# Side sums taken by turns on VectorE, a narrower last convolution block on TensorE, and other rounds with bank halves

## The chip, the cores and the metric

The kernel runs on one core of a Trainium2 chip. The metric is the time of one execution on the device in microseconds (us), lower is better. Three runs of the kernel before were timed; their median is 510.24 us.

## What is computed

A causal convolution along the sequence, with softmaxed taps of 7 per head (8 heads of 24 columns, D = 192), feeds a multiplicative feed-forward network:

```python
w = softmax(weight)                                   # H=8 heads, K=7 taps
out = np.einsum('hk,bskhg->bshg', w, x_unf)           # x_unf[t, k] = x[t - 6 + k], zeros ahead of a batch
a = out @ w1                                          # 192 -> 1024
b = out @ w2
return ((a * b) @ w3) @ w_out                         # 1024 -> 1024 -> 192
```

There are 8 batches of 3904 tokens, 31232 rows in all. The kernel multiplies `w3 @ w_out` once, so a row needs two products to 1024 columns, an elementwise product, and one product back to 192.

## The kernel before, in words

**Streams, rounds, stages.** The rows are cut into two streams of 15616, which share the 128 partitions (64 columns of D each). A round R is 512 tokens of both streams; there are 31. Three rounds make a stage (`phases`): first the *first products* of its three rounds, then their *second products*, two a round (one for each stream), six in all. Stage 0 holds rounds 0 to 2, stage 9 the first products of 27 to 29 and the second ones of 27, a last stage the rest.

- A first product (`first_product`) has eight steps. In each, TensorE makes `pa` and `pb` (six matmul pairs of 64 rows each, line 633), ScalarE copies `pa` to `asb` (line 640), and VectorE multiplies `asb` with `pb` to `abT` (line 643).
- A second product (`second_product`) is 32 matmuls of 128 rows (line 685) into one pair of banks, `ops`; ScalarE copies it to `osb` (line 690) and SyncE's queue sends it out.
- All PSUM tiles are pairs of banks from one ring of four, so the third `pb` of a stage waits until VectorE has read the first.

**Halves.** In stages 3, 6, 7 and 8 (`halves`) the two second products of a round are made by `half_rows` in matmuls of 64 rows, two at a time (line 664): the first half of both products, then the second half of both, with the banks changed over. Between the halves a no-operation on VectorE (`passed`, line 674) waits for the first half's last matmul, and the second half waits for it. So both products of a round are done late in it: the first after three quarters.

**Where the convolution is done.** D is three column groups k of 64. The tokens of rounds 2q+1 and 2q+2 form pair q. For q in `SIDE` (4, 5, 8, 9, 12, 13, 14) all three groups are convolved aside: VectorE, and for some halves GpSimd, multiplies and adds seven shifted copies, group by group. In `PART` (10 and 11) group 0 alone is made aside. All else TensorE convolves with banded matrices (`conv`, line 345), ScalarE copies the result out (line 355), it is stored to DRAM and read back transposed. Blocks 4, 5 and 6 are convolved between the second products, in units of up to two heads (`units`, `places`): four units in stage 0, four in stage 2, three (heads 2 to 7 of block 6) in stage 5. A unit of two heads is 32 matmuls.

**A side task** is (q, k, tokens). Its rows are cast to bf16 by GpSimd's DMA queue (`side_cast`), read back transposed on SyncE's queue (`side_transpose`, five buffers in turn), scaled by the tap of shift 1 on ScalarE (`side_first`, line 520; the *first scaling*), and then VectorE adds the six other shifts (`side_sums`, line 538; the *sums*), each 1024 elements wide, or 768 for q = 14. There are two accumulators: task i takes `acc_of[i % 2]`, so its first scaling waits for the last sum of task i - 2. Sums all add to the task's own accumulator. If a batch starts within the task, the sums are split there.

**GpSimd's half tasks** (`POOL_AT`) work alike on 512 tokens; where a stage has two of them, ScalarE does their first scalings (`pool_first`, line 571) in the stage before, around its fifth second product.

**The order.** VectorE, ScalarE and the queues take their instructions in program order. A planner spreads the sums over the stages: `rooms` says how many a stage takes, `steps` is the list of all sums, task by task, and `chain[p]` becomes stage p's list, with each first scaling put at a number n. `side_steps(p, n, ...)`, called after each second product, issues what is due. So VectorE's queue holds in a stage 24 products of line 643, then the stage's sums, then the next stage's products. ScalarE's holds 24 copies of line 640, then evictions of line 690, evictions of the convolution, first scalings and GpSimd's first scalings in program order, then the next stage's copies. In halves, the sums are also portioned out around VectorE's no-operations (`limit`).

Of the kernel before, what the change touches and what calls it, by code (L numbers as in the profile page):

```python
# [16 lines left out]
def kernel(  # L17
# [32 lines left out]
    PART = {10: (0,), 11: (0,)}  # L50
# [418 lines left out]
    def half_of(q, h):  # L469
# [4 lines left out]
               5: ((8, 2, 1), (11, 0, 0)), 6: ((12, 2, 0), (11, 0, 1)), 7: ((12, 2, 1),),  # L474
# [11 lines left out]
    def side_tiles():  # L486
# [8 lines left out]
        for i, q in enumerate(SIDE):  # L495
            side_of[q] = (a if i % 2 == 0 else b)[:, 0:NP * 2 * CH].rearrange(
                "p (k t) -> p k t", k=NP)
# [26 lines left out]
    def side_sums(i):  # L524
# [4 lines left out]
        def job(d, last):  # L529
            def run():  # L530
# [4 lines left out]
                for lo, hi in [(t0, t1)] if last else \  # L535
# [3 lines left out]
                        out=side_of[p][:, k, o:o + t1 - t0] if last else a,  # L539
# [3 lines left out]
        size = (t1 - t0) / (2 * CH)  # L543
# [10 lines left out]
    def part_tile():  # L554
        t = work.tile([128, XN], BF16, tag="xb", bufs=5, name="side")
        o = 0
        for q, ks in PART.items():
            n = len(ks) * 2 * CH
            side_of[q] = t[:, o:o + n].rearrange("p (k t) -> p k t", k=len(ks))
            o += n  # L560
# [14 lines left out]
    def pool_sums(lane, own, p, k, half):  # L575
        _, _, t0, starts = pool_half(p, k, half)

        def job(d):
            def run():
# [9 lines left out]
                if d == 0:  # L589
                    o = half * CH  # L590
                    nc.gpsimd.tensor_tensor(out=side_of[p][:, k, o:o + CH], in0=acc, in1=tmp,
# [9 lines left out]
    def operand(R, k, rs):  # L601
        if beside(phase_of(R), k):
            t0 = R * CH - side_span(phase_of(R))[0]
            return side_of[phase_of(R)][rs, k, t0:t0 + width(R)]
# [68 lines left out]
    def passed(mm):  # L673
        relay = nc.vector.nop()
# [125 lines left out]
    starts, chain, begun, room, p = {}, {}, set(), 0, -1  # L800
    for i, cost, f in steps:
        while room < cost:
# [4 lines left out]
        if i not in begun:  # L807
            begun.add(i)
            starts[p].append(i)
            n = max(p == 0, int(at) // 2 - 1, -(-ends.get(i - 2, 0) // 2))  # L810
# [4 lines left out]
        ends[i] = at  # L815
    for p in starts:
        for i in starts[p]:
            assert i < 5 or p < 2 or max(v for v in chain if chain[v][0][0] <= i - 5) <= p - 1

    def side_steps(p, n, state, limit=100):  # L820
        items = chain.get(p, [])
        done = sum(items[v][3] for v in state)
        for v, (i, at, f, cost) in enumerate(items):
            if at is not None and at <= n and v not in state:
# [221 lines left out]
```

## Time and profile before

| | |
|---|---|
| median of 3 runs | 510.24 us (509.89 the lowest) |
| the profiled execution | 510.52 us, of which its span is 508.8 |
| granted TensorE clock | 0.999 |

The rows of the page and of the chain of waits that matter are shown in the prediction. In the page's first part each engine has its busy time, its share of the span and its number of instructions; the chain shows what ended last, followed back. In a timeline each row is a start, a length, the engine, the line, what is written and read, and a count where like instructions follow each other; a bracket gives the idle time before, and who ended it. All times are in us from the start of the span.

### The profile page before, as it was taken

The page shows a single profiled execution, that of the slowest core. Times are in us where ns is not written, and L with a number is a line of the kernel's source. Part 1 is how long each engine was busy: PE and PEld are TensorE (multiplying, and loading weights), DVE is VectorE, ACT ScalarE, POOL GpSimd, SP SyncE. Part 2 cuts the span into 40 slices and gives each one's busy share as a digit, 9 for nine tenths or more (in the row PEclk, how much of TensorE's full clock was granted, in tenths as well). Part 3 has the DMA queues.
Part 4 walks back from the last instruction along what each step waited for, and adds up shares of the span by engine and source line. Part 5 has one row for each costly group of instructions (what it writes and reads, how often), then busy time and mean ns, then how long its engine had stood idle before and what let it go on. Part 6 is the DMA issues. An engine that isn't in the chain of part 4 may idle for free.

```text
span 508.8 us, 15240 instructions
## 1 busy us (share of the span) xinstructions
PE 503.7 (99%) x6500; PEld 336.5 (66%) x6500; DVE 446.3 (88%) x402; ACT 349.1 (69%) x390; POOL 255.7 (50%) x340
## 2 busy tenths in 40 slices
PE   8999999999999999999999999999999999999997
PEld 4546865595569557845874596569457855975697
DVE  7898769999999799999999998999999999999930
ACT  6786667746779776577567778763776477457752
POOL 8875201332890799499879944992371056000000
PEclk9999999999999999999999999999999999999999
DMA  9999979999969858970997097619402500240025
GB/s 136 152 173 157 176 151 180 151 164 173 175 41 165 150 144 112 227 120 13 92 234 109 4 166 142 130 23 182 111 1 72 162 1 1 65 125 1 1 66 156
DMA packets 161121, 58.57 MB, mean 115 GB/s; under 512 B 116896, under 2 KB 161052, under 8 KB 161052
## 3 DMA queue, kind: packets, MB, share of 16 engines
q0 software_dynamic: 74784, 17.37, 37.9%
q1 hardware_dynamic: 86107, 40.12, 37.2%
q8 instruction: 51, 0.84, 0.6%
q14 instruction: 19, 0.15, 0.1%
q10 hardware_dynamic: 160, 0.10, 0.1%
HBM read 35.02 MB, written 34.85 MB: 137 GB/s over the span
## 4 chain that ended last, share of the span: by engine, by line
PE 98%; ACT 0%; DVE 0%; issue 0%
PE pa L633 31%; PE pb L633 31%; PE ops L685 19%; PE ops L664 12%; PE cps L345 1%; PE wps L757 1%; PE warm L246 1%; PE tps L420 0%; PE ops L710 0%; DVE abT L643 0%; PE tps L435 0%; PE cps L375 0%; ACT asb L640 0%; ACT convo L355 0%; PE bps L305 0%
## 5 line engine op out<-in xcount | busy, mean ns | idle before, releaser
L643 DVE TENSOR_TENSOR abT<-asb,pb 128x1024 bf16<-128x1024 bf16 x240 | 292.6, 1220 | 28.9 <-ACT asb L640 12.8
L640 ACT CAST asb<-pa 128x1024 bf16<-128x1024 f32 x244 | 247.0, 1012 | 64.0 <-PE pa L633 63.8
L633 PEld LDWEIGHTS <-wn 64*128 64x128 bf16 x1488 | 138.8, 94 | 81.3 <-issue 0.9
L633 PEld LDWEIGHTS <-ws 64*128 64x128 bf16 x1488 | 130.4, 94 | 70.7 <-issue 0.9
L633 PE MATMUL pb<-xT,wn 64*128 64x512 bf16 x376 | 103.7, 376 | 0.0
L633 PE MATMUL pa<-xT,ws 64*128 64x512 bf16 x376 | 103.5, 376 | 0.0
L690 ACT COPY osb<-ops 128x768 f32<-128x768 f32 (+1 forms) x61 | 48.4, 795 | 80.0 <-PE ops L685 42.9
L633 PE MATMUL pa<-xT,wn 64*128 64x512 bf16 x376 | 102.9, 376 | 0.1
L633 PE MATMUL pb<-xT,ws 64*128 64x512 bf16 x376 | 102.2, 376 | 0.0
L633 PE MATMUL pb<-side,wn 64*128 64x512 bf16 (+1 forms) x368 | 100.5, 369 | 0.0
L685 PE MATMUL ops<-W_sb,abT 128*128 128x192 bf16 x1168 | 99.5, 246 | 0.0
L633 PE MATMUL pa<-side,wn 64*128 64x512 bf16 (+1 forms) x368 | 99.3, 369 | 0.0
L633 PE MATMUL pa<-side,ws 64*128 64x512 bf16 (+1 forms) x368 | 99.3, 369 | 0.0
L685 PEld LDWEIGHTS <-abT 128*128 128x128 bf16 x1168 | 95.4, 98 | 4.6 <-issue 4.6
L633 PE MATMUL pb<-side,ws 64*128 64x512 bf16 (+1 forms) x368 | 98.2, 369 | 0.0
L538 DVE SCALAR_TENSOR_TENSOR acc<-raw,wC,acc 128x1024 f32<-128x1024 bf16 (+2 forms) x70 | 84.5, 1208 | 2.3 <-PE ops L664 0.2
L596 POOL TENSOR_TENSOR acc<-acc,tmp 128x512 f32<-128x512 f32 (+6 forms) x60 | 70.3, 1176 | 4.3
L584 POOL TENSOR_TENSOR tmp<-acc,wC 128x512 f32<-128x512 bf16 x66 | 68.5, 1038 | 3.5
L664 PE MATMUL ops<-W_sb,abT 64*128 64x192 bf16 x1536 | 64.2, 243 | 0.4 <-issue 0.4
L664 PEld LDWEIGHTS <-abT 64*128 64x128 bf16 x1536 | 63.5, 94 | 1.5 <-issue 0.6
L951 POOL COPY pace<-abT 1x2 bf16<-1x2 bf16 x28 | 4.9, 174 | 109.4 <-DVE abT L643 109.3
L506 POOL DMA_DIRECT2D rows_c<-in_x_dram x58 | 40.7, 710 | 6.3 <-issue 5.5
(85 smaller groups left out, 247.0 us busy)
## 6 DMA issues: line engine op xcount, KB each, us to landing
out_dram<-osb SPq DMA_DIRECT2D x54, 384.0 KB
xb<-in_x_dram POOLq DMA_DIRECT2D x16, 240.0 KB, 7.3
out_dram<-osb SPq DMA_DIRECT2D x12, 192.0 KB
rows_c<-in_x_dram POOLq DMA_DIRECT2D x14, 130.0 KB, 6.7
rows_c<-in_x_dram POOLq DMA_DIRECT2D x14, 128.0 KB, 5.9
xb<-in_x_dram POOLq DMA_DIRECT2D x6, 228.0 KB, 8.8
w3b<-in_moe_w_dram POOLq DMA_DIRECT2D x4, 256.0 KB, 5.6
w3b<-in_moe_w_dram POOLq DMA_DIRECT2D x8, 128.0 KB, 4.9
```

Source lines behind the costliest of these rows:

```text
L246: nc.tensor.matmul(t[:, j % 2, 0:wd].rearrange("p (a c) -> p a c", c=128), zeros, zeros.unsqueeze(1).to_broadcast([128, wd // 128, 128]), ...
L345: nc.tensor.matmul(o.rearrange("p (w g) -> p w g", g=wd)[:, :, c - c0:c1 - c0], Aband[group(r, e), h, :], xb[group(r, e), s:s + m, c:c1], ...
L506: nc.gpsimd.dma_start(out=rows_c[lo:t1, k, r * Q:r * Q + Q], in_=x_rows[r * TS + lo:r * TS + t1, k * Q:k * Q + Q])
L538: nc.vector.scalar_tensor_tensor(out=side_of[p][:, k, o:o + t1 - t0] if last else a, in0=raw[:, HALO + lo - t0 - d:HALO + hi - t0 - d], sc ...
L584: nc.gpsimd.tensor_tensor(out=acc if d == 1 else tmp, in0=pool_raw[lane][:, HALO - d:HALO - d + CH], in1=wC[:, k, K - 1 - d:K - d].to_broa ...
L596: nc.gpsimd.tensor_tensor(out=a, in0=a, in1=tmp[:, lo - t0:hi - t0], op=ALU.add)
L633: nc.tensor.matmul(p[:, r, f * N:f * N + N], w_of(i, k, r)[rs, ft * 128:(ft + 1) * 128], operand(R, k, rs), start=(k == 0), stop=(k == NP ...
L640: nc.scalar.copy(out=asb[:, :, 0:per * N], in_=pa[:, :, 0:per * N])
L643: nc.vector.tensor_tensor(out=ab[:, f0, :, 0:N], in0=asb[:, :, 0:N], in1=pb[:, :, 0:N], op=ALU.mult)
L664: mm = nc.tensor.matmul(ops[:, a, g * D:g * D + D], ab[rs, jt, r, q * 128:(q + 1) * 128], W_sb[rs, jt, :], start=(turn == 0 and g == 0 and ...
L685: nc.tensor.matmul(ops[:, g // 2, (g % 2) * D:(g % 2) * D + D], ab[:, jt, r, g * 128:(g + 1) * 128], W_sb[:, jt, :], start=(jt == 0), stop ...
L690: nc.scalar.copy(out=osb.rearrange("p (a g) d -> p a (g d)", g=2), in_=ops[:, 0:ng // 2, 0:2 * D])
```

## The change

- `PART` holds groups 0 and 1 of pairs 10 and 11: tasks (10, 1) and (11, 1) go to VectorE, twelve sums more. Block 6 is then convolved by TensorE for heads 5 to 7 alone, in units of two heads and one, in places 1 and 3 of stage 5.
- The second half of (13, 2) goes from VectorE to GpSimd, in stage 7, which then has two half tasks.
- The sums are no longer listed task by task: the even and the odd tasks make two lists, which are taken by turns, by what each has spent. `rooms` is new (15 in stage 2, 14 in stage 5, else about 13), and a first scaling's number n comes from 1.2 us a sum and 2.66 a second product.
- The bank turn's no-operation (`passed`) moves from VectorE to ScalarE; `side_steps` loses its `limit`.
- Halves are used in stages 6 to 9 and in the last round of stages 2 and 5; not in stage 3.
- In halves, GpSimd's first scalings are issued after the eviction of the fifth second product, no longer ahead of it.
- The side results of pairs 10 and 11 take two tiles (`part_tile(3)` in stages 3 and 6).

```diff
-    PART = {10: (0,), 11: (0,)}
+    PART = {10: (0, 1), 11: (0, 1)}
...
-               5: ((8, 2, 1), (11, 0, 0)), 6: ((12, 2, 0), (11, 0, 1)), 7: ((12, 2, 1),),
+               5: ((8, 2, 1), (11, 0, 0)), 6: ((12, 2, 0), (11, 0, 1)), 7: ((12, 2, 1), (13, 2, 1)),
...
-    for q in SIDE:
-        for k in range(NP):
+    for q in sorted(SIDE + tuple(PART)):
+        for k in PART.get(q, range(NP)):
...
-        size = (t1 - t0) / (2 * CH)
+        size = (t1 - t0 + 130) / (2 * CH + 130)
...
     def passed(mm):
-        relay = nc.vector.nop()
+        relay = nc.scalar.nop()
...
-    places = {0: (1, 2, 3, 4), 2: (0, 1, 2, 3), 5: (0, 1, 3)}
-    rooms = (6, 12, 12, 12, 12, 12, 12, 11.25, 12)
-    steps = [(i, cost, f) for i in range(len(tasks)) for cost, f in side_sums(i)]
-    late_sum = max(v for v, (i, _, _) in enumerate(steps) if tasks[i][:2] == (12, 0))
+    places = {0: (1, 2, 3, 4), 2: (0, 1, 2, 3), 5: (1, 3)}
+    rooms = (6, 12, 15, 13, 13, 14, 13, 12.7, 13)
+    lines = [[(i, cost, f) for i in range(c, len(tasks), 2) for cost, f in side_sums(i)]
+             for c in range(2)]
+    spent, steps = [0, rooms[0]], []
+    while any(lines):
+        c = min((c for c in range(2) if lines[c]), key=lambda c: (round(spent[c], 2), c))
+        steps.append(lines[c].pop(0))
+        spent[c] += steps[-1][1]
+    late_sum = max(v for v, (i, _, _) in enumerate(steps) if tasks[i][:2] == (14, 0))
...
-            n = max(p == 0, int(at) // 2 - 1, -(-ends.get(i - 2, 0) // 2))
+            n = max(p == 0, int((1.2 * ends.get(i - 2, -1) + 1.2) / 2.66))
...
+    units = [(b, h, min(n, H - h)) for b, h, n in units]
...
-        if p == 3:
-            part_tile()
+        if p in (3, 6):
+            part_tile(3)
...
-        halves = p in (3, 6, 7, 8)
-        side_steps(p, 0, state, 0 if halves else 100)
+        side_steps(p, 0, state)
         for n, (R, r) in enumerate((R, r) for R in ends for r in range(NS)):
+            halves = p in (6, 7, 8, 9) or p in (2, 5) and R == ends[-1]
             if halves and r == 0:
                 opss = [banks("ops") for _ in range(NS)]
                 mms = [half_rows(R, i, opss[i], 0) for i in range(NS)]
-                relays = []
-                for i in range(NS):
-                    side_steps(p, n, state, 2 * n + i)
-                    relays.append(passed(mms[i]))
+                relays = [passed(mm) for mm in mms]
                 for i in range(NS):
                     half_rows(R, i, opss[i], 1, relays[i])
-                side_steps(p, n, state, 2 * n + 2)
-                side_steps(p, n + 1, state, 2 * n + 4)
-            own_first = n == 4 and len(pool_from.get(p, ())) > 1
-            if own_first and halves:
-                for lane, t in enumerate(pool_from[p]):
-                    pool_first(lane, *t)
...
-                second_product(R, r, results if p == 0 else None, opss[r])
-            if own_first and not halves:
+                second_product(R, r, results if p == 0 else None, opss[r] if halves else None)
+            if n == 4 and len(pool_from.get(p, ())) > 1:
                 for lane, t in enumerate(pool_from[p]):
                     pool_first(lane, *t)
             if n in places.get(p, ()):
                 convolve(p)
-            side_steps(p, n + 1, state, 2 * n + 2 if halves and n < 5 else 100)
+            side_steps(p, n + 1, state)
```

With these lists the stages hold (task.shift; F is a first scaling, with its n): stage 2: F4, F3 at 0, tasks 4 and 3 by turns (12 sums), F6 at 5, 6.2, F5 at 5, 5.2, 6.3. Stage 3: nine sums of 5 and 6, F8 at 4, 8.2, F7 at 4, 7.2, 8.3, 7.3. Stage 4: eight of 8 and 7, F10 at 3, 10.2, F9 at 4, 9.2, 10.3, 9.3, 10.4. Stage 5: seven of 9 and 10, F12 and F11 at 3, seven of 12 and 11. Stage 6: five of 11 and 12, F14 and F13 at 2, eight of 14 and 13. Stage 7: four of 14 and 13, F16 at 1, 16.2, F15 at 2, eight of 15 and 16. Stage 8: 15.6, 16.0, F18 at 1, 18.2, 15.0, 18.3, F17 at 2, ten of 17 and 18. Tasks 3 to 18 are now (5,0), (5,1), (8,0), (8,1), (9,0), (9,1), (9,2), (10,1), (11,1), (12,0), (12,1), (13,0), (13,1), (14,0), (14,1), (14,2).

More of the change, by code (lines that the diff above doesn't have):

```diff
@@ L538, in run @@
                     nc.vector.scalar_tensor_tensor(
[L539 removed]
+                        out=side_of[p, k][:, o:o + t1 - t0] if last else a,
                         in0=raw[:, HALO + lo - t0 - d:HALO + hi - t0 - d],
@@ L815, with side_steps @@
         ends[i] = at
+        ended[i] = p
     for p in starts:
         for i in starts[p]:
[L818 to L820 removed]
+            assert i < 5 or p < 2 or ended[i - 5] <= p - 1
+    for i, (q, k, _, _) in enumerate(tasks):
+        n = SIDE.index(q) - 2 if q in SIDE else -1
+        assert n < 0 or ended[i] >= stage_of(2 * SIDE[n] + 2)
+    def side_steps(p, n, state):
         items = chain.get(p, [])
[L822 removed]
         for v, (i, at, f, cost) in enumerate(items):
[L824 to L825 removed]
+            if at is not None and at > n:
+                break
+            if v not in state:
                 state.add(v)
                 f()
[L828 to L836 removed]
     def seq(*fs):
@@ L967 @@
         raws = starts.get(p + 1, ())
-        late = [i for i in raws if p == 0 or len(lanes) > 1 or i >= 5 and chain[p][0][0] <= i - 5]
+        late = [i for i in raws if p == 0 or len(lanes) > 1 or i >= 5 and ended[i - 5] >= p]
         if p > 1:
```

38 lines of the change are left out of this document (13 added, 25 removed).

## The prediction, made before the change was run

> **What bounds the kernel now.** The page comes first: busy shares, then the chain that ended last.
>
> ```profile
> PE 503.7 (99%) x6500; PEld 336.5 (66%) x6500; DVE 446.3 (88%) x402; ACT 349.1 (69%) x390; POOL 255.7 (50%) x340
> PE 98%; ACT 0%; DVE 0%; issue 0%
> ```
>
> TensorE is the path; whatever it is spared is gain, whatever it must wait for is loss. VectorE at 88% is the nearest. The chain in order of time (start, length, what) gives the stages; I call the six second products of a stage P0 to P5, T the start of P0, and F the start of the next stage's first products.
>
> ```profile
> 101.31 15.95 PE ops L685 x192
> ...
> 148.44 2.75 PE ops L685 x32
> 151.19 0.35 PE cps L345 x32
> ...
> 160.84 5.39 PE ops L685 x64
> 166.23 0.75 PE pa L633 x6
> 166.98 0.65 PE pb L633 x6
> ...
> 169.57 0.43 PE pb L633 x3
> ...
> 197.42 14.11 PE ops L664 x342
> 211.53 0.38 issue
> 211.91 1.91 PE ops L664 x42
> ...
> 292.03 2.75 PE ops L685 x32
> 309.35 0.75 PE pa L633 x6
> 340.54 15.84 PE ops L664 x384
> ```
>
> See: a stage with whole rows takes 15.95 (stage 1), in halves 15.84 (stage 6); whole rows begin and end with a step of 0.10 (0.75 against 0.65, 2.75 against 2.65), halves don't. Stage 2 with four convolutions takes 166.23 - 148.44 = 17.79, stage 5 with three 309.35 - 292.03 = 17.32. Stage 3, in halves, has 0.38 of issue in it.
>
> How near VectorE and ScalarE are to holding TensorE up is read at a stage's turn. VectorE's timeline at the end of stage 1, and at both ends of stage 2:
>
> ```profile
> 102.88 6.56 DVE L538 SCALAR_TENSOR_TENSOR acc<-raw,wC,acc 128x1024 f32<-128x1024 bf16 x5
> 109.48 1.28 DVE L538 SCALAR_TENSOR_TENSOR side<-raw,wC,acc 128x1024 bf16<-128x1024 bf16 x1
> 110.68 6.56 DVE L538 SCALAR_TENSOR_TENSOR acc<-raw,wC,acc 128x1024 f32<-128x1024 bf16 x5
> 119.09 1.22 DVE L643 TENSOR_TENSOR abT<-asb,pb 128x1024 bf16<-128x1024 bf16 x1 [0.53 <-ACT asb L640]
> ...
> 150.02 6.56 DVE L538 SCALAR_TENSOR_TENSOR acc<-raw,wC,acc 128x1024 f32<-128x1024 bf16 x5
> 168.13 3.75 DVE L643 TENSOR_TENSOR abT<-asb,pb 128x1024 bf16<-128x1024 bf16 x3 [2.19 <-ACT asb L640]
> ```
>
> See: within a task a sum starts (6.56 - 1.28)/4 = 1.32 after the one whose result it adds to; the first sum of the other task starts 110.68 - 109.48 = 1.20 after the last of this one. So 1.20 is what a sum costs that doesn't build on its predecessor. Sums begin at T + 1.58 (150.02 - 148.44). The first product of stage 3 (call it M) starts at F + 1.90 (168.13 - 166.23). TensorE needs M's banks for its third pb, at F + 3.34 (169.57); M takes 1.22, so it may start at F + 2.10. **The reserve is 0.20 us**: what M is later than that, TensorE waits.
>
> ScalarE, in stage 2 and, below the dots, in stage 3 (halves):
>
> ```profile
> 156.83 1.19 ACT L520 ACTIVATE acc<-raw,wC 128x1024 f32<-128x1024 bf16 x1
> 157.88 0.83 ACT L690 COPY osb<-ops 128x768 f32<-128x768 f32 x1
> 161.22 1.83 ACT L355 CAST convo<-cps 128x960 bf16<-128x960 f32 x2
> 163.63 0.80 ACT L690 COPY osb<-ops 128x768 f32<-128x768 f32 x1 [0.58 <-PE ops L685]
> 164.32 1.34 ACT L571 ACTIVATE acc<-acc,wC 128x512 f32<-128x512 bf16 x2
> 166.27 0.80 ACT L690 COPY osb<-ops 128x768 f32<-128x768 f32 x1 [0.61 <-PE ops L685]
> 167.03 1.01 ACT L640 CAST asb<-pa 128x1024 bf16<-128x1024 f32 x1
> ...
> 201.42 0.80 ACT L690 COPY osb<-ops 128x768 f32<-128x768 f32 x1 [2.55 <-PE ops L664]
> 208.71 1.33 ACT L571 ACTIVATE acc<-acc,wC 128x512 f32<-128x512 bf16 x2
> ```
>
> See: start to start, a first scaling of a task (L520) takes 1.05, an eviction 0.69, GpSimd's two scalings (L571) 0.62 each. ScalarE has a free second between its last eviction and the next asb only because nothing else stands there. In halves P0 is ready at 201.42 - 197.42 = 4.00 after T, not 2.75: both products of a round come late in it.
>
> **The change, part by part.**
>
> *TensorE, less.* Stage 5 has units of 32 and 16 matmuls in place of three of 32. Three cost 17.32 - 15.95 = 1.37, 0.46 each (0.35 of matmuls, 0.1 of step); the two cost 0.46 and 0.18 + 0.10: **-0.63**. Halves: stage 3 loses them (15.84 to 15.95, and a step of 0.10: +0.21), stage 9's one round gains as much, 0.2, the last rounds of stages 2 and 5 about 0.1 each: -0.2. Stage 3's 197.42 to 213.82 is 16.40, 0.56 above a stage of halves; the chain names no engine for it, so I take it as gone: -0.56 (bounds -0.56 and 0). Together **-1.4**, bounds -0.8 and -1.4. ScalarE is spared evictions in stage 5; it isn't the path there.
>
> *VectorE, more.* Twelve sums for (10,1) and (11,1), less six half sums of (13,2). Taken by turns each costs 1.20; 13 cost 15.6, as much as 12 before (11 x 1.32 + 1.20 = 15.7). Tasks of 768:
>
> ```profile
> 438.29 1.02 DVE L538 SCALAR_TENSOR_TENSOR side<-side,wC,acc 128x768 bf16<-128x768 bf16 x1
> 439.22 5.23 DVE L538 SCALAR_TENSOR_TENSOR acc<-raw,wC,acc 128x768 f32<-128x768 bf16 x5
> ```
>
> 0.93 by turns, (5.23 - 1.02)/4 = 1.05 in a row. A batch starts within (10,1), so five of its sums are split (960 and some 60 columns): by 1.20 and 0.93, 1.05 ns a column and 0.12 a start, 0.13 more each, and one memset of about 0.1.
>
> The rooms and the two lists give the order. Stage 1 holds tasks 2 and 1 by turns, twelve sums, ending with reserve. **Stage 2** is the one to follow: 15 sums, of which the last three (6, 5, 6) need the first scalings of tasks 6 and 5, which stand on ScalarE after P4's eviction and GpSimd's two scalings and ahead of P5's eviction. Its last round is now in halves. From T: the fourth convolution ends at 12.40 (160.84); P4 at 12.40 + 0.10 + 3.96 = 16.46, P5 and F at 17.78. ScalarE: eviction of P4 16.50, GpSimd's scalings 17.19 and 17.81, task 6 at 18.43, task 5 at 19.48, eviction of P5 20.53, first asb 21.22 to 22.23. VectorE has done twelve sums at 1.58 + 14.4 = 15.98 and stands idle till task 6's scaling has ended, 18.43 + 1.19 = 19.62; the three sums take it to 19.62 + 3.60 = 23.22. M starts there, at F + 5.44: **TensorE waits 5.44 - 2.10 = 3.3**. Bounds: 1.7 from ScalarE alone (the third pa, due F + 2.70, needs the asb that ends at F + 4.45), 3.7 if the three sums go 1.32 apart. What is late next: nothing, M's follower needs only its own asb, and 24 products a stage give the rest back.
>
> Stage 3 (13 sums, whole rows): task 8's scaling at 11.34, task 7's at 12.50, M at 17.33 < 15.95 + 1.90: nothing. Stage 4 (13, four of the first ones for tasks 8 and 7 by turns, three split): task 9's scaling ends 13.0, five sums and 0.3 of splits take M to 18.1 = F + 2.15: 0.1. Stage 5 (14): VectorE, with two splits, would let M start at 18.75, but P4 is ready only at 15.37 (halves), so ScalarE has P4 15.41, two scalings, P5 17.34, asb 18.03 to 19.04: M at F + 2.38 (F 16.69): 0.3. Stage 6 (all halves): the same queue, P4 14.56, P5 16.49, asb 17.18 to 18.19, F 15.84: 0.3. In stage 3 before (208.71 above) GpSimd's scalings stand ahead of the fifth eviction, where they hide; the change puts them behind it. Stage 7: nothing. Stage 8: task 18's scaling waits for P0, task 17's for the sum of task 15 at 7.88; then ten sums of 0.94 to 18.29, F 15.84 + 0.1: 0.35 with the bank turn below. Small ones **1.05**, bounds 0 and 2.
>
> *The bank turns on ScalarE.* VectorE no longer has them between its sums. On ScalarE one stands behind task 13's scaling in stage 6 and task 17's in stage 8; these wait for VectorE (7.66 and 7.88 after T), and TensorE needs the turn at 5.28 + 2.64 = 7.92. 0 to 0.1 each, counted above. In stage 2 it stands behind the fourth convolution's evictions (163.05 - 148.44 = 14.61 at the latest), needed at 15.1: hidden, by 0.5.
>
> *GpSimd and queues.* Eleven more instructions in stage 7, where two half tasks now go one after the other (their first scalings are the new ones on ScalarE in stage 6). Stage 3's first products show that load:
>
> ```profile
> 166.20:197.30 31.10, 31.10 (x291) 15.53 (x292) 27.60 (x23) 24.52 (x25) 27.33 (x25) 1.00 0.65 133
> ```
>
> 27.33 of 31.10 busy on POOL, TensorE without a gap; the result is read in stage 9, a stage later. Nothing; without that cover some 1. POOL's queue issues four more casts; stage 1 issues eight for tasks in place of four, with the loads of block 5 behind them, which are used a stage later; SP has four transposes more for the two tasks and four fewer of TensorE's columns, and the late ones wait for sums that end before the stage does, with only outputs behind them. Nothing.
>
> **The sum.** -1.4 + 3.3 + 1.05 = +2.95. The profiled execution took 510.52 (its span 508.8 and 1.7 around it), 0.28 above the median of 510.24; 510.52 + 2.95 = **513.5**, by the bounds 510.52 - 1.4 + 1.7 = 510.8 to 510.52 - 0.8 + 3.7 + 2.0 = 515.4.
>
> **Rivals.** (1) *The cover holds*: no wait on ScalarE grows into TensorE, the saving stays: 510.52 - 1.4 = 509.1. For it: the bound is TensorE and before, a late first scaling (156.83) cost nothing. Against: the reserve is 0.20, and the order of ScalarE's queue is written in the program.
>
> (2) *Turns don't help*: a sum costs 1.32 (0.94 sums 1.05) whatever stands before it. Then stage 2 waits 3.7, stage 3 0.8 (M at 18.8), stage 4 1.3, stage 5 1.7, stage 6 1.2, stage 8 1.6 (the queues above, with 1.32 in place of 1.20): 10.3; 510.52 - 1.4 + 10.3 = 519.4. This is the one that can end slower: 0.01 of a sum's pitch is (10.3 - 4.35)/12 = 0.5 us, and 2% (10.2) is passed from a pitch of 1.35. Against it stand the 1.20 above and the 0.93. The Trainium skill (VectorE: DVE Perf Modes, section "The DRAIN you can't avoid") says that the next operation doesn't start until the pipe is empty, and that this can't be skipped by leaving out semaphores; though the section lets an operation that isn't held start earlier; by the first rule it is this rival, 519.4. The trace disagrees with it where the task changes, 1.20 against 1.32.
>
> (3) *Only stage 2's wait is smaller*, since VectorE's last three sums don't hold M but ScalarE does: 1.7 in place of 3.3, 511.9. It lies within my bounds.
>
> **How the numbers follow.** My forecast with (3): 0.72, 510.8 to 515.4. Rival (1) 0.12, rival (2) 0.11 (a third of it beyond 2%), anything else, such as a transfer that comes late, 0.05. The range 510.3 to 517.5 holds the first and the near sides of the others, some 0.8. A measurement here tells about 2% from no change, that is 500.0 and 520.4: faster 0.01, same 0.94, slower 0.05.
>
> **What would show it.** In the profile after: stage 5's second products 16.7 long; sums 1.20 apart; at the turn from stage 2 to 3, some 3 us in which the chain leaves TensorE for L520, L538 and L643, M about 5 us behind F, an L520 that starts some 18 us after T. Wrong if sums come 1.3 apart (rival 2), if that turn has no gap (rival 1), or if gaps stand in the middle of second products (bank turns).

## The result, and the profile after

The changed kernel takes 515.89 us (median of 5 runs, 514.59 to 517.32) against 510.24 before: a ratio of 1.0108, 95% interval [1.0088, 1.0128]. The record has five executions of the kernel before, 509.89, 509.89, 510.24, 510.65 and one of 879.8, which is no part of the ratio. The result is within 2% of before, 2.4 us slower than the stated 513.5, inside the range of 510.3 to 517.5 and outside the narrower bounds of the forecast itself, 510.8 to 515.4. The profiled execution is the longest of the five, 517.32 us; its span is 515.6 and its granted clock 1.0.

Its page, busy shares and the chain that ended last (in the changed kernel line numbers from the second products on are 2 lower: L683 for L685, L662 for L664, L631 for L633, L638 for L640, L641 for L643, L569 for L571, L688 for L690):

```profile
PE 503.8 (98%) x6452; PEld 341.7 (66%) x6452; DVE 449.8 (87%) x414; ACT 349.2 (68%) x389; POOL 271.6 (53%) x350
PE 82%; DMA 7%; POOL 4%; DVE 3%; issue 2%; ACT 1%; ACTq 0%; POOLq 0%; DVEq 0%
```

See: TensorE's busy time is unchanged (503.8 against 503.7, although the matmuls are fewer), and the chain that was TensorE for 98% now leaves it for 18% of the span. The DMA and POOL shares come from the first 60 us (below); the shares of VectorE and ScalarE are the turns and, for the most part, stage 8, where the chain follows the sums from 446.61 on. The chain from stage 2 to stage 6, in order of time (start, length, what):

```profile
151.14 2.75 PE ops L683 x32
...
163.54 4.08 PE ops L662 x96
...
168.34 1.29 ACT acc L569 x2
169.63 0.99 issue
...
170.92 0.73 issue
...
172.44 0.92 ACT asb L638
...
174.34 1.23 DVE abT L641
...
175.61 0.82 PE pb L631 x6
...
203.63 15.95 PE ops L683 x192
...
270.05 0.82 PE pb L631 x6
...
314.83 0.65 PE pa L631 x6
```

See: stage 3 is down from 16.40 to 15.95. At the turn from stage 2 to 3 the chain goes through GpSimd's scalings, the first scalings (mostly under "issue" here; ScalarE's timeline below has them), an eviction, a copy and a product before TensorE resumes at 175.61.

Where TensorE resumes after a wait, the chain's next piece of six takes 0.82 in place of 0.65, at 175.61 and 270.05 alike. That is no cost of resuming: in the timeline the next six matmuls begin at 176.25, 0.64 behind 175.61, as in an unbroken run. Matmuls overlap (each takes 0.38 here, and the next pair starts 0.22 behind), and the chain counts a piece from the end of the one ahead; in an unbroken run that is 0.16 behind the start of its first matmul. This touches the prediction's reserve. The third `pb` of stage 3's first products in the timeline of the kernel before, and the first `pa` and the third `pb` behind stage 5 in the changed kernel:

```profile
169.41 0.38 PE L633 MATMUL pb<-side,wn 64*128 64x512 bf16 x1
```

```profile
314.67 0.38 PE L631 MATMUL pa<-side,wn 64*128 64x512 bf16 x1
...
318.49 0.37 PE L631 MATMUL pb<-side,wn 64*128 64x512 bf16 x1 [0.42 <-DVE abT L641]
```

See: before, TensorE needed M's banks at 169.41, not at the chain's 169.57, and M ended at 168.13 + 1.22 = 169.35. So **the reserve was 0.02 rather than 0.20**, if 0.04 pass between M's end and the matmul that waits for it (318.45 to 318.49). Without a wait the third `pb` starts 3.25 after the first `pa` (169.41 - 166.16 before); behind stage 5 it starts 318.49 - 314.67 = 3.82 after it, 0.57 late, with M at 317.22, F + 2.39. So behind halves M may start at F + 1.82; behind the whole rows of stage 4, where M at F + 2.08 makes 0.16, at F + 1.92. The prediction has F + 2.10 for all.

ScalarE at that turn (T = 151.14, start of the stage's second products; F = 168.93, where the last of them ends in TensorE's timeline):

```profile
167.65 0.80 ACT L688 COPY osb<-ops 128x768 f32<-128x768 f32 x1 [1.90 <-PE ops L662]
168.34 1.33 ACT L569 ACTIVATE acc<-acc,wC 128x512 f32<-128x512 bf16 x2
169.58 1.14 ACT L520 ACTIVATE acc<-raw,wC 128x1024 f32<-128x1024 bf16 x1
170.62 1.14 ACT L520 ACTIVATE acc<-side,wC 128x1024 f32<-128x1024 bf16 x1
171.66 0.78 ACT L688 COPY osb<-ops 128x768 f32<-128x768 f32 x1
172.34 3.00 ACT L638 CAST asb<-pa 128x1024 bf16<-128x1024 f32 x3
```

VectorE in the same stage:

```profile
152.71 12.04 DVE L538 SCALAR_TENSOR_TENSOR acc<-raw,wC,acc 128x1024 f32<-128x1024 bf16 x10
...
170.75 1.28 DVE L538 SCALAR_TENSOR_TENSOR acc<-raw,wC,acc 128x1024 f32<-128x1024 bf16 x1 [3.60 <-ACT acc L520]
171.95 1.28 DVE L538 SCALAR_TENSOR_TENSOR acc<-side,wC,acc 128x1024 f32<-128x1024 bf16 x1
173.15 1.28 DVE L538 SCALAR_TENSOR_TENSOR acc<-raw,wC,acc 128x1024 f32<-128x1024 bf16 x1
174.34 3.48 DVE L641 TENSOR_TENSOR abT<-asb,pb 128x1024 bf16<-128x1024 bf16 x3
```

See: task 6's scaling starts 169.58 - 151.14 = 18.44 after T, VectorE stands idle 3.60 us for it, and the first product M starts at 174.34, F + 5.41. Sums by turns are (12.04 - 1.28)/9 = 1.20 apart.

By stage (from the first matmul of a stage's second products to the next one's, so a stage's number holds its second products and the next first products), the profiled execution stands to that of before so:

| us | stage 0 | 1 | 2 | 3 | 4 | 5 | 6 | 7 | 8 | 9 and last |
|---|---|---|---|---|---|---|---|---|---|---|
| predicted | 0 | 0 | +3.2 | -0.35 | +0.1 | -0.43 | +0.3 | 0 | +0.35 | -0.2 |
| measured | **+2.79** | 0 | +3.61 | -0.44 | +0.17 | **-0.09** | **+0.60** | -0.05 | +0.50 | -0.24 |

All but stage 0 make +4.06, where the prediction has +2.95. Of the last column 0.10 is stage 9; the other 0.14 isn't the change's, as two more profiles of the kernel before (e10 and e11) have -0.33 and -0.32 in the last stage.

### The profile page after: what moved, and what is told of

The parts are those of the page before. It is cut to its first block, busy times and chain, and to the rows that moved or that the text cites. A ratio compares the mean times of both kernels' runs of the same rounds, so it can differ in the third digit from the quotient of the medians.

```text
span 515.6 us, 15163 instructions
## 1 busy us (share of the span) xinstructions
PE 503.8 (98%) x6452; PEld 341.7 (66%) x6452; DVE 449.8 (87%) x414; ACT 349.2 (68%) x389; POOL 271.6 (53%) x350
## 4 chain that ended last, share of the span: by engine, by line
PE 82%; DMA 7%; POOL 4%; DVE 3%; issue 2%; ACT 1%; ACTq 0%; POOLq 0%; DVEq 0%
PE pb L631 27%; PE pa L631 26%; PE ops L683 18%; PE ops L662 10%; DMA xb<-in_x_dram 5%; DVE acc L538 2%; POOL xb L165 1%; POOL ws L227 1%; DMA w3b<-in_moe_w_dram 1%; DVE abT L641 1%; POOL w3b L736 1%; PE cps L345 1%; ACT asb L638 1%; DVE side L538 1%; ACT acc L520 0%
## 5 line engine op out<-in xcount | busy, mean ns | idle before, releaser
L641 DVE TENSOR_TENSOR abT<-asb,pb 128x1024 bf16<-128x1024 bf16 x240 | 291.9, 1220 | 26.6 <-ACT asb L638 11.6
L638 ACT CAST asb<-pa 128x1024 bf16<-128x1024 f32 x244 | 246.7, 1012 | 65.6 <-PE pa L631 65.1
L631 PEld LDWEIGHTS <-wn 64*128 64x128 bf16 x1488 | 138.9, 94 | 77.2 <-issue 0.6
L631 PEld LDWEIGHTS <-ws 64*128 64x128 bf16 x1488 | 129.5, 94 | 74.4 <-issue 6.8
L631 PE MATMUL pb<-side,wn 64*128 64x512 bf16 (+1 forms) x400 | 108.7, 370 | 4.1 <-DVE abT L641 2.5
L631 PE MATMUL pa<-side,wn 64*128 64x512 bf16 (+1 forms) x400 | 106.8, 370 | 0.1
L631 PE MATMUL pa<-side,ws 64*128 64x512 bf16 (+1 forms) x400 | 105.6, 370 | 0.0
L631 PE MATMUL pb<-side,ws 64*128 64x512 bf16 (+1 forms) x400 | 103.7, 370 | 0.0
L688 ACT COPY osb<-ops 128x768 f32<-128x768 f32 (+1 forms) x61 | 48.2, 791 | 81.9 <-PE ops L683 45.8
L683 PE MATMUL ops<-W_sb,abT 128*128 128x192 bf16 x1168 | 99.0, 246 | 0.0
L683 PEld LDWEIGHTS <-abT 128*128 128x128 bf16 x1168 | 95.6, 98 | 4.1 <-issue 4.1
L631 PE MATMUL pb<-xT,wn 64*128 64x512 bf16 x344 | 97.0, 376 | 0.0
L631 PE MATMUL pa<-xT,wn 64*128 64x512 bf16 x344 | 96.3, 376 | 0.1
L631 PE MATMUL pa<-xT,ws 64*128 64x512 bf16 x344 | 96.3, 376 | 0.0
L631 PE MATMUL pb<-xT,ws 64*128 64x512 bf16 x344 | 95.1, 376 | 0.0
L538 DVE SCALAR_TENSOR_TENSOR acc<-raw,wC,acc 128x1024 f32<-128x1024 bf16 (+1 forms) x75 | 88.0, 1226 | 6.1 <-ACT acc L520 5.9
L594 POOL TENSOR_TENSOR acc<-acc,tmp 128x512 f32<-128x512 f32 (+1 forms) x65 | 76.7, 1183 | 4.7
L582 POOL TENSOR_TENSOR tmp<-acc,wC 128x512 f32<-128x512 bf16 x72 | 74.8, 1039 | 4.4
L662 PE MATMUL ops<-W_sb,abT 64*128 64x192 bf16 x1536 | 64.6, 243 | 0.1
L662 PEld LDWEIGHTS <-abT 64*128 64x128 bf16 x1536 | 63.4, 94 | 1.4 <-ACTq L672 0.3
```

The source lines that it names most:

```text
L538: nc.vector.scalar_tensor_tensor(out=side_of[p, k][:, o:o + t1 - t0] if last else a, in0=raw[:, HALO + lo - t0 - d:HALO + hi - t0 - d], sc ...
L582: nc.gpsimd.tensor_tensor(out=acc if d == 1 else tmp, in0=pool_raw[lane][:, HALO - d:HALO - d + CH], in1=wC[:, k, K - 1 - d:K - d].to_broa ...
L594: nc.gpsimd.tensor_tensor(out=a, in0=a, in1=tmp[:, lo - t0:hi - t0], op=ALU.add)
L631: nc.tensor.matmul(p[:, r, f * N:f * N + N], w_of(i, k, r)[rs, ft * 128:(ft + 1) * 128], operand(R, k, rs), start=(k == 0), stop=(k == NP ...
L638: nc.scalar.copy(out=asb[:, :, 0:per * N], in_=pa[:, :, 0:per * N])
L641: nc.vector.tensor_tensor(out=ab[:, f0, :, 0:N], in0=asb[:, :, 0:N], in1=pb[:, :, 0:N], op=ALU.mult)
```

## The experiments

The theory to be tested: the loss is made at the stages' turns, where ScalarE's queue and VectorE's last sums reach past the end of the second products, and TensorE's saving is real. Its rivals: sums by turns cost more than 1.20; the number of sums in stage 2 decides by itself; something that the prediction priced at nothing (GpSimd, the DMA queues) costs the rest.

### e1: stage 2 with whole rows

```diff
-            halves = p in (6, 7, 8, 9) or p in (2, 5) and R == ends[-1]
+            halves = p in (6, 7, 8, 9) or p == 5 and R == ends[-1]
```

> The last round of stage 2 in whole rows again, all else as in the changed kernel. Queue theory (TensorE waits at the turn from stage 2 to 3 because ScalarE takes P4's eviction, GpSimd's two scalings and two first scalings one after the other, and VectorE's last three sums come behind them): P4 is ready 1.3 us earlier, the first scaling starts near 17.05 after T, M at 21.85 instead of 23.2, so that turn's wait falls by 1.3 to 1.4 us (3.5 to about 2.1) and the kernel by about 1.2. Rival (the number of sums, 15 in place of 12, holds M): the wait stays at 3.5 and the kernel where it is. Stage 0: in the changed kernel's profile a convolution waited 2.3 us for a load; if that belongs to the run and not to the change, it is of another size here.

Measured: 514.43 us (513.33 to 514.97), ratio 1.0078 [1.0063, 1.0093]. Stage 2's turn falls from +3.61 to +2.29, and M from F + 5.41 to F + 4.09. So the late P4 of a halves round, which holds up everything that ScalarE has behind it, makes 1.3 us of the wait; the number of sums is unchanged. But the profiled execution lost 2.02 us at a new place, in the first products that follow stage 1. The chain there:

```profile
122.99 6.39 issue
129.52 1.04 POOL acc L582
...
144.25 0.13 POOL pace L950
...
144.40 1.02 ACT asb L638
...
146.72 0.82 PE pb L631 x6
```

See: the chain runs through GpSimd. Its `pace` copies keep its queue in step with the rounds; the one at 144.25 reads two elements of the first `asb` of the stage's third round. GpSimd was late, so the copy was late, and ScalarE could not write that `asb` buffer again until the copy had read it; VectorE and TensorE stood behind. GpSimd's half task began at 129.52. Before it began here (GpSimd's timeline of the kernel before, then of e1):

```profile
125.31 1.04 POOL L584 TENSOR_TENSOR acc<-acc,wC 128x512 f32<-128x512 bf16 x1 [2.00 <-PE pb L633]
```

```profile
129.51 1.04 POOL L582 TENSOR_TENSOR acc<-acc,wC 128x512 f32<-128x512 bf16 x1 [6.53 <-PE pa L631]
```

The input of the half task comes through two queues, and on SyncE's it stands behind the transposes of the side tasks. Before, and in e1, which has the changed kernel's order:

```profile
115.90 5.96 SPq L515 DMA_TRANSPOSE raw<-rows_c  x4
...
121.96 1.20 SPq L568 DMA_TRANSPOSE acc<-rows_c  x1
```

```profile
114.48 7.59 SPq L515 DMA_TRANSPOSE raw<-rows_c  x4
122.17 2.51 SPq L515 DMA_TRANSPOSE side<-rows_c  x2
124.78 1.20 SPq L566 DMA_TRANSPOSE acc<-rows_c  x1
```

See: stage 2 now starts four tasks, so three of them are transposed ahead of the half task (x4 and x2, two transposes a task) where two were, and it is issued 2.8 us later. From the end of that issue to GpSimd's start it takes 3.5 us in e1 (125.98 to 129.51) and 3.5 to 3.9 in e5 and e2; in the profiles of the changed kernel, e3 and e4 it takes 1.7 to 1.8, and those have no such wait. So the new order makes the half task late, and some 2 us more at its start, which come in some executions, make TensorE wait. What these 2 us are isn't shown. (The changed kernel's own profile has the start at 129.62, but all of it runs 2.7 us later from stage 0 on.)

### e2: GpSimd's scalings ahead of the fifth eviction in halves, as before

```diff
+            own_first = n == 4 and len(pool_from.get(p, ())) > 1
+            if own_first and halves:
+                for lane, t in enumerate(pool_from[p]):
+                    pool_first(lane, *t)
...
-            if n == 4 and len(pool_from.get(p, ())) > 1:
+            if own_first and not halves:
```

> In halves, GpSimd's first scalings stand ahead of the fifth eviction again, all else as in the changed kernel. Queue theory: everything behind them on ScalarE moves up by 1.24 us; the turn from stage 2 to 3 waits 2.3 instead of 3.5, those from 5 to 6 and from 6 to 7 lose most of their 0.6; together -2.0 to -2.3 us. Rival (the number of sums): no turn changes, 0.

Measured: 514.31 us (median of three executions, 512.27 to 514.48; a fourth took 520.89, at a granted clock of 0.993), ratio 1.0067 [1.0044, 1.009]. By stage against the changed kernel's profile: stage 2 -1.17, stage 5 -0.37, stage 6 -0.59, together -2.1. The placing of two scalings of 0.62 behind an eviction that comes late costs that much, and +1.89 at GpSimd's copy stood in this profile too.

### e3: three sums left out

```diff
-        chain.setdefault(p, []).append((i, None, f, cost))
+        chain.setdefault(p, []).append((i, None, f if p != 2 or i < 5 else lambda: None, cost))
```

> Leaves out the last three sums of stage 2 (two of task 6, one of task 5), but keeps their first scalings, all else as in the changed kernel. Queue theory with ScalarE as well as VectorE in the way: M then starts right behind the first asb, at F + 4.5 instead of F + 5.4, the wait is 2.5 instead of 3.5. Rival (VectorE's sums alone hold M): the wait goes altogether, -3.5. Rival (ScalarE alone holds it): no change.

Measured: 514.54 us (513.55 to 515.85), ratio 1.0092 [1.0075, 1.0109]. Stage 2 stands at +2.72 in place of +3.61, and M starts at F + 4.51, when ScalarE's first `asb` has ended (F + 4.43). So 0.9 of the wait is VectorE's three sums, and the rest ScalarE's own queue. The prediction's lower bound of 1.7 was too low for that: it looked at the third `pa`, but M itself can't start ahead of the first `asb`'s end, F + 4.45 in its own working, which is 2.6 past the F + 1.82 of above.

### e4: sums task by task, as before

```diff
-    spent, steps = [0, rooms[0]], []
-    while any(lines):
-        c = min((c for c in range(2) if lines[c]), key=lambda c: (round(spent[c], 2), c))
-        steps.append(lines[c].pop(0))
-        spent[c] += steps[-1][1]
+    steps = sorted(lines[0] + lines[1], key=lambda s: s[0])
...
-        if p in (3, 6):
+        if p in (3, 5):
```

> The sums in the old order, task by task, with the changed kernel's rooms; the second side tile of pair 11 is taken in stage 5, as task (11,1) ends there. If a sum costs 1.32 behind its own task and 1.20 behind another (theory): sums 1.32 apart, M in stages 2, 3, 4, 5 and 6 later than the reserve by about 1.4, 0.6, 0.6, 1.9 and 1.2 with the restart, 5.7 in all, so the time is about that of the changed kernel, 514 to 517, though stage 2 waits 2 us less, since a first scaling is due earlier there. If turns don't matter (1.20 either way): waits of 1 us in all, about 511. If the old order costs 1.32 and turns bring more than I think: above 518.

Measured: 513.68 us (513.42 to 513.70), ratio 1.0065 [1.005, 1.008]; the expectation is missed at its lower end. VectorE's timeline at stage 2:

```profile
150.02 6.56 DVE L538 SCALAR_TENSOR_TENSOR acc<-raw,wC,acc 128x1024 f32<-128x1024 bf16 x5
156.62 1.28 DVE L538 SCALAR_TENSOR_TENSOR side<-raw,wC,acc 128x1024 bf16<-128x1024 bf16 x1
...
165.62 3.92 DVE L538 SCALAR_TENSOR_TENSOR acc<-side,wC,acc 128x1024 f32<-128x1024 bf16 x3
```

See: (6.56 - 1.28)/4 = 1.32 again. The order sets the pitch, as predicted: 1.20 by turns, 1.32 in a row. Yet the slower order loses no time as a whole: against the changed kernel's profile it loses 0.35 to 0.55 at each turn of stages 3 to 6, and saves 2.2 at stage 2's and 0.6 at stage 8's. In stage 2 the last three sums are of one task (the row x3), so one first scaling stands late on ScalarE in place of two.

### e5 and e6: the changed kernel again, and with the half task first

e5 is the changed kernel unchanged. e6 puts the half task of stage 2 at the head of both queues:

```diff
-    casts += [(p if p < 3 else p - 1, f) for p, v in pool_from.items() for q, k, h in v
-              for f in side_cast(None, (q, k, *half_of(q, h)))]
+    lent = [(p if p < 3 else p - 1, f) for p, v in pool_from.items() for q, k, h in v
+            for f in side_cast(None, (q, k, *half_of(q, h)))]
+    casts = [c for c in lent if c[0] == 1] + casts + [c for c in lent if c[0] != 1]
...
-        if p > 1:
+        if p > 0:
...
-        if p == 1:
-            pool_transpose(0, *pool_from[p][0])
```

> The changed kernel once more, to stand beside the next two on the same chip. By the stages of its first profile it takes 514.5 without the wait in stage 0. Theory (GpSimd): stage 1 now casts four tasks in place of two, the half task of stage 2 comes last in its queue, its first multiplication starts later, and where it starts over some 11 us after the first products of stage 2, TensorE waits there for up to 2 us; so the runs scatter between 514.5 and 516.5. Rival (stage 0's load is what scatters): runs up to 517.3, and the profile shows a wait in stage 0 or none at all.

> As the changed kernel, but in stage 1 the casts and the transpose of GpSimd's half task go ahead of those of the side tasks. Theory (GpSimd): its first multiplication in stage 2 starts less than 8 us after the first products there, the wait of 2 us never comes, the runs stand within 1 us and the median is 514.5, about 1.4 below the changed kernel's. Rival (stage 0's load, or anything else): the scatter and the median stay as in the changed kernel.

Measured on one chip: e5 517.27 us (515.79 to 518.24), ratio 1.0134 [1.0119, 1.015]; e6 514.77 (514.40 to 515.29), ratio 1.0091 [1.0078, 1.0104]. The medians stand 2.5 us apart, and most of the scatter is gone. Not all of that is the half task. Two of e5's four executions (517.73 and 518.24) have a granted clock of 0.997; the profiled one of them starts stage 0's second products 1.95 late (last section). The other two, at 1.0, are 515.79 and 516.81, 1.0 and 2.0 above e6. GpSimd's first multiplication in e5, and in e6:

```profile
131.51 1.04 POOL L582 TENSOR_TENSOR acc<-acc,wC 128x512 f32<-128x512 bf16 x1 [6.25 <-DVE abT L641]
```

```profile
123.93 1.04 POOL L582 TENSOR_TENSOR acc<-acc,wC 128x512 f32<-128x512 bf16 x1 [0.56 <-PE pb L631]
```

The waits of e5 in that stretch have ScalarE's copy behind GpSimd's `pace` (us in total, times, longest); in e6 no such row is left:

```profile
ACT asb L638 <- POOL pace L950: 2.0, 1, 2.0
```

This shows the second cause: in the new order the half task comes too late. Where the wait comes it costs 1.7 us (e5), 1.9 (e2) or 2.0 (e1); three of the five profiles that have it in full (the changed kernel, e1, e2, e3, e5) show it, and in how many executions it comes isn't measured.

### e8: the bank turn back on VectorE

```diff
-        relay = nc.scalar.nop()
+        relay = nc.vector.nop()
```

> As the changed kernel, but the bank turn's no-operation is on VectorE again, behind whatever sums stand ahead of it in the program. Queue theory: in stages 5 to 8 TensorE waits in the middle of its second products till those sums are done, about 4 us in stage 5, 8 to 10 in each of stages 6, 7 and 8, in all 25 to 35 us, about 545. Rival (the turn is free wherever it stands): 514 to 517.

Measured: 552.09 us in one run, some 42 above the kernel before. With whole lists of sums ahead of it the no-operation holds TensorE in the middle of the second products of stages 5 to 8. So its move to ScalarE is needed with this order of sums. It isn't free there: of the 0 to 0.1 stated for each of two stages, stage 6 shows 0.02, but stage 8's second products take 16.10 in the changed kernel where they took 15.84, and its waits there have

```profile
PEld L662 <- ACTq L672: 0.3, 1, 0.3
```

which is TensorE, in the middle of the second products, waiting for the bank turn on ScalarE. Part of the 7 more than expected in e8 is the clock (below).

### e7, e9, e12: everything put right

All three have stage 2 in whole rows, the half task first (as e6), and GpSimd's scalings ahead of the fifth eviction in halves (as e2); they differ in stage 2's lists and in where GpSimd's two scalings stand there: behind the third eviction in e7, ahead of the first in e9 (`n == 0`), ahead of the third in e12 (`n == 2`). e7 also takes 13 sums in stage 1 and 14 in stage 2. e12 against the changed kernel, besides e1's and e6's edits:

```diff
-    rooms = (6, 12, 15, 13, 13, 14, 13, 12.7, 13)
+    rooms = (6, 12, 15, 13, 13, 14, 13, 12.95, 13)
...
-            n = max(p == 0, int((1.2 * ends.get(i - 2, -1) + 1.2) / 2.66))
+            n = max(p == 0, int((1.2 * ends.get(i - 2, -1) + 1.2) / 2.66)) - (p == 2 and i > 4)
...
+            own_first = n == (2 if p == 2 else 4) and len(pool_from.get(p, ())) > 1
+            if own_first and (halves or p == 2):
+                for lane, t in enumerate(pool_from[p]):
+                    pool_first(lane, *t)
...
-            if n == 4 and len(pool_from.get(p, ())) > 1:
+            if own_first and not halves and p != 2:
```

> The changed kernel with what the runs so far point to: stage 2 in whole rows, GpSimd's two scalings after its third product there, and ahead of the fifth eviction in halves; task 5's scaling a step earlier; rooms 13 in stage 1, 14 in stage 2, 12.95 in stage 7; the half task first in stage 1. Queue theory: no wait at the turns from 1 to 2, 2 to 3, 3 to 4 and 6 to 7, 0.2 from 4 to 5, 0.4 from 5 to 6, 0.2 in or after stage 8; the sum of the stages is 0.9 below the kernel before, 509.2 to 509.9 where that takes 510.2. Rival (the number of sums holds M): 513 or more.

e7 measured: 511.13 us (510.08 to 513.73, 12 runs), ratio 1.0025 [1.001, 1.004]; missed by 1.2 to 1.9. GpSimd's scalings held a convolution's eviction, and TensorE, for 0.54 in stage 2, and the profiled execution (513.55) had a late load in stage 0, worth 3.0.

> Stage 2 with whole rows; GpSimd's two scalings at its very start, where ScalarE stands idle 1.33 us ahead of the first eviction (e7 had them behind the third eviction, where 0.54 of wait came); the scalings of tasks 6 and 5 behind the fourth convolution, 12 sums in stage 1 and 15 in stage 2 as in the changed kernel; the rest as e7. My theory (the time is what ScalarE's queue and GpSimd's half task take at stage 2's turn and in the small turns, and TensorE's saving is real): by stage against before, stages 1 and 2 nothing to +0.2, stage 3 -0.44, stage 4 +0.17, stage 5 -0.46, stages 9 and 10 -0.4, so about -1.0 where no load is late at the start: 509.0 to 509.6, ratio about 0.998. The rival (the change costs something at the start, through loads, in most executions): 511 to 513 with a scatter like e7's, and 1 to 3 us in stage 0 of the profile.

e9 measured: 517.88 us (516.59 to 519.16), ratio 1.0151 [1.0126, 1.0177]; missed by over 8. The idle second at the head of the stage is of no use to the scalings, because their input isn't there yet. ScalarE in e9:

```profile
156.74 1.33 ACT L569 ACTIVATE acc<-acc,wC 128x512 f32<-128x512 bf16 x2 [6.01 <-DMA acc<-rows_c]
```

See: the scalings wait 6.01 us for their transposes, and all evictions of the stage stand behind them. Stage 2 takes 8.06 more than before; TensorE's clock, 0.50 from 160.5 to 163.5, has a part in it. It is the failed step of the prediction once more, by my own hand: an instruction moved up a queue, and its input's way through the other queues not followed.

> e9 with GpSimd's two scalings of stage 2 ahead of the third eviction instead of the first: in e9 ScalarE waited 6.01 us there for their transposed input, which landed 8.5 us after the stage's start, and here the place comes 8.6 after it. My theory: no wait for the input, at most 0.3 in stage 2, nothing in stage 1, stage 3 -0.44, stage 4 +0.17, stage 5 -0.46, stages 9 and 10 -0.3: about -0.8 to -1.1 in the executions without a late load at the start, median 509.2 to 510.0, lowest run near 509. The rival, late loads at the start in most executions: a median over 510.5 with a scatter of 2 to 3 us, as e7 had.

e12 measured: 510.19 us (509.76 to 512.14, 12 runs), ratio 0.9998 [0.9982, 1.0014], the same as before; the median is 0.2 over what I expected, the lowest run 0.8. Stage 2 kept +0.54: in the chain the transposes land at 157.14, and the scalings, an eviction and a convolution's evictions behind them hold TensorE. So with the causes in the queues removed the 5.65 us are back, while the change's saving is eaten by such remains: e12's profiled span is 508.6, those of e10 and e11 are 508.0 and 508.1. No version that I ran beats the kernel before.

### e10, e11: the kernel before again

> The kernel before, profiled once more, for the waits at the start. If a late load in stage 0 is a matter of the single execution, one of these two profiles may show some of it (0.4 to 3 us in stage 0, in TensorE's wait for the block that it convolves), and the times stay at 510 to 511 with few above. If it belongs to the change, stage 0 is 17.85 long in both, as in the first profile of before.

> The same once more: a second profile of the kernel before, to count how often a load is late in stage 0. Expected as above.

Measured: 510.05 us (509.67 to 510.45) and 510.46 (509.81 to 512.20), both the kernel before. Neither profile has a wait in stage 0. But the 0.56 of stage 3, which the prediction counted as the change's gain, isn't always there. Stage 3 in e10:

```profile
197.51 15.84 PE ops L664 x384
213.35 0.65 PE pa L633 x6
```

See: 15.84 without a piece of issue, as any stage in halves; in e11 the stage takes 16.09, 0.25 over, with 0.07 of issue. So the stall comes and goes, and its 0.56 belong to the one execution that I worked from.

## Why the prediction was right or wrong

**Right: the mechanism of the largest term.** Task 6's scaling was to start 18.43 after T and started at 18.44; M was to start at F + 5.44 and started at F + 5.41; the turn was to cost 3.3 with 0.1 saved, and the stage cost 3.61. e1 and e2 show that ScalarE's queue behind a late P4 makes much of it (1.3 and 1.2 come back), e3 that VectorE's three sums hold the last 0.9. Rival (1) falls with this gap, rival (3) with M's place.

**Right: 1.20 a sum by turns.** 1.20 after the change, 1.32 in e4. So rival (2) falls, and with it the strict reading of the Trainium skill (VectorE: DVE Perf Modes, section "The DRAIN you can't avoid"), by which no order could shorten the pitch: the trace disagrees with it, by 0.12 us a sum, and fits the section's exception, by which an operation that isn't held starts earlier.

**Right: the saving on TensorE**, less the 0.56 of stage 3, which is in some executions of the kernel before and not in others (0.56, 0.25 and 0 in three profiles). Without it 0.83 was stated. Measured are 0.66 in stage 5 (17.33 to 16.67), 0.10 in stage 2, about 0.2 for stage 9's round in halves, and about 0.2 lost in stage 3: some 0.76 in all. Counting the 0.56 as gained was right for the profiled execution by luck, since a second profile of before could have been without it.

**Mis-sized: the small turns.** 1.05 was stated. Stage 5 measures -0.09 where -0.43 was due, stage 6 +0.60 for +0.3, stage 8 +0.50 for +0.35, stage 4 +0.17 for +0.1, stage 2 +3.61 for +3.2: 1.3 too little in all, partly offset by stages 3 and 9. Most of it is the reserve. Read from the chain's 169.57 it let M start at F + 2.10; the timeline gives F + 1.92 behind whole rows and F + 1.82 behind halves. That is 0.18 too much at the turn of stage 4 and 0.28 at those of stages 2, 5 and 6, 1.0 in all; M itself came where it was forecast (F + 5.41 for 5.44, and behind stage 5 F + 2.39 for 2.38). In stage 8 the bank turn takes 0.26 where 0 to 0.1 was stated, from the same misreading: task 17's scaling started 7.91 after T, just ahead of the 7.92 at which TensorE was said to need the turn, but by the starts of the matmuls it was due 0.2 earlier. So one of the prediction's own signs of being wrong, a gap in the middle of second products, is there once.

**Wrong: the step "GpSimd and queues … Nothing".** It said that stage 1 issues eight casts for tasks in place of four, with only the loads of block 5 behind them, and that the late transposes have only outputs behind them. The half task of stage 2 stands behind both. It came 2.8 us later on SyncE's queue (e1), GpSimd's in-order copy that reads `asb` came late with it, and ScalarE, VectorE and TensorE waited 1.7 to 2.0 us in the profiles of e1, e2 and e5. In e6, which moves only that half task, the wait is gone. With it and the small turns, 513.5 becomes about 516.6, and the median is 515.89: not every execution has the wait, as the first profile after shows. That 515.89 still lies in the stated range is luck in part: the room above 515.4 was left for the near side of rival (2), which did not happen, and not for a wait at GpSimd.

**Not foreseen, and open: late loads at the start.** The profiled execution after has +2.79 in stage 0. Its chain there:

```profile
41.74 9.17 DMA xb<-in_x_dram
...
51.19 9.14 DMA xb<-in_x_dram
...
60.38 0.39 PE cps L345 x21
```

See: GpSimd's queue issues a load when an earlier one has landed (at 32.07 it had waited 2.27 for one), so one late landing passes down the queue to the columns that TensorE convolves at 60.38. e7's profile has the same (+3.0). e5's starts 1.95 later for another reason, a first load that TensorE waits for at 7.22 and a slow clock behind it (last section). The three profiles of the kernel before have no wait in stage 0, nor have e1, e2, e3, e6, e9 and e12 (e4 has 0.18). The order of that queue is the same in all of these kernels up to there. Beside e12, 2 of 17 runs of the kernel before took 512.86 and 513.0 and the rest at most 511.57; 3 of e12's 12 took 511.9 to 512.1. So longer executions aren't the change's alone, though no profile of a long execution of the kernel before shows that a load makes them; whether the change makes late loads more frequent isn't settled.

## What to carry to other kernels

When a change adds work to one engine, follow every in-order queue past the added or moved instruction, the DMA queues included, down to whoever reads what stands behind it: here three queues each had something behind them that "nothing" forgot. Look at the turn between two stages for the reserve in tenths of a microsecond: there a late eviction costs nearly its whole delay, while inside a stage much of it is hidden (not all: 0.54 in e7 and e12). Read that reserve from the first matmul that needs the banks, in the timeline; the chain's pieces begin at the end of the piece ahead. And profile the kernel before more than once before a stall of half a microsecond is booked as gain.

## What the runs showed of the hardware

A wait of TensorE can cost more than itself. The two waits at stage 2's turn in the changed kernel, 1.62 and 1.38 long, left the clock alone, and so did 1.9 in its stage 0. In e8 TensorE stood still from 349.9 to 352.6; the stretches (bounds, length, busy of PE, PEld, DVE, ACT, POOL, granted clock, DMA share, GB/s):

```profile
349.90:352.60 2.70, 0.01 (x2) 0.00 (x0) 2.70 (x4) 0.00 (x0) 2.70 (x5) 1.00 1.67 107
352.60:354.60 2.00, 1.96 (x30) 1.92 (x32) 2.00 (x2) 0.00 (x0) 1.33 (x2) 0.62 2.25 143
354.60:356.00 1.40, 1.40 (x22) 1.35 (x20) 0.31 (x1) 0.80 (x1) 0.00 (x0) 0.50 2.22 141
356.00:357.20 1.20, 1.20 (x28) 1.18 (x26) 0.00 (x0) 0.05 (x1) 0.00 (x0) 0.79 0.50 82
```

See: for some 4 us after the wait the granted clock is 0.5 to 0.8. e8's chain has the price:

```profile
352.64 4.49 PE ops L662 x64
...
366.42 9.88 PE ops L662 x192
```

At 15.84 for 384 these would take 2.64 and 7.92: 1.85 and 1.96 us more (the second follows a stop of 6.7). Another stop in e8, the 2.4 ahead of 311.7, is followed by a clock of 0.61. The Trainium skill (TensorE: Matmul & The Clock Gate, section "What's actually happening") says that the clock is halved after an idle window of about 3.4 us and restored after a busy one; the halving and the length of the slow stretch agree, while here 2.4 us without a matmul were enough.

The length of one stop doesn't decide by itself. At the start of e5 TensorE waited only 0.83 us for a load, and the clock went down behind it:

```profile
7.22 0.74 PE L345 MATMUL cps<-xb,Aband 32*32 32x120 bf16 x61 [0.83 <-DMA xb<-in_x_dram]
```

```profile
9.00:10.00 1.00, 1.00 (x10) 0.88 (x9) 0.02 (x1) 0.86 (x2) 1.00 (x2) 0.50 1.18 174
```

See: the granted clock is 0.50 from 9.0 to 11.5, and the first `pa` starts at 10.50 in place of 8.93 before. What else decides isn't shown.
